# A product tile in two parts, the softmax four superblocks ahead, and other places for the x loads, in a dynamic convolution followed by a gated two-matmul block

## The chip, the cores and the metric

One core of a Trainium2 chip. The metric is the device time of one execution in microseconds (us); of the kernel before there are three runs.

## What is computed

The input x has 8 sequences of 4096 tokens with 192 channels; weight_gen has, for each token and each of 8 heads, 7 weights. A softmax is taken over the 7 weights; each output channel is the weighted sum of the channel at this token and the six before it (zeros before the start of a sequence). The result, 32768 tokens by 192, goes through a matmul to 2048 channels, the function h - tanh(h), and a matmul back to 192.

```python
w = np.exp(weight_gen - max); w = w / sum(w)
x_pad = concatenate([zeros((B, 6, D)), x], axis=1)
out = einsum('bshk,bskhg->bshg', w, x_unf)     # x_unf: 7 shifted copies of x_pad
h = out.reshape(B * S, D) @ w_in
return (h - tanh(h)) @ w_out
```

## The kernel before

The tokens are cut into 32 superblocks (SBs) of 1024: partition p holds 8 tokens in a row (J = 8) and, ahead of them, the six before (HALO). NSB = 4 SBs make a sequence, so SBs 0, 4, 8, ... 28 start one; their first partition has no tokens before it and gets zeros in its halo.

Each SB goes through these steps:

- `load_wg` (L96) and `load_x` (L106) bring the softmax weights (128 x 448 numbers) and x (128 rows of 14 x 192 numbers, 10,752 bytes each) through SP's queue. `rows(p0, p1, ...)` issues the load of partitions p0 to p1; `no_halo` (L123) fills the halo of partition 0 with zeros.
- `softmax_exp` (L144, ACT), `softmax_sum` (L157, DVE) and `softmax_norm` (L172, DVE) give the weights `wsm`.
- `products` (L221) multiplies x by the weights for the seven taps. In the steady part this is all on GpSimd (POOL): taps 0 and 1, then 2 to 5, then 6, into one tile `pr` with two buffers.
- `dma_sum` (L213) is an accumulating DMA that POOL issues: it adds taps 3 to 5 onto 0 to 2 (the first sum, issued between the second and the third product, SUM_FIRST). For the SBs in TWO_SUMS a second one (`second_sum`, L289) follows, behind the first product of the next SB. SBs 2 to 4 (PART) have one sum of two taps; SBs 0 and 1 have none.
- `conv_sums` (L294, TensorE) transposes and adds what is left of the taps: four groups of 24 small matmuls after one sum, two groups after two sums. `conv_out` (L322, ACT) copies the result out.
- `gemm1` (L349): sixteen steps f; in each the first matmul, tanh on ACT (L367), subtraction on DVE (L368). `out_stream` (L376) is the second matmul, whose pairs are spread over the steps of the next loop, and `store_out` (L402) copies and stores its result.

The order of the work is written out by hand: the main loop (L568) goes over n = 1 to 31 and, within it, over the steps f = 0 to 15. In loop n the first matmul of SB n, the second matmul of SB n-1, the transposes of SB n+1 (at f = 13 and 14), the products of SB n+2 (issued at f = 1), the softmax of SB n+3 and the loads of x of SB n+3 (at f = X_AT = 7, ordered behind that step's subtraction) and of the weights of SB n+4 stand. Each engine runs its own instructions in this order; a DMA queue likewise issues in order, and an issue that waits holds those behind it. Buffers are given by pools: x_t, the softmax tiles and `pr` have two each.

Of the kernel before, what the change touches and what calls it, by code (L numbers as in the profile page):

```python
# [8 lines left out]
FP32 = mybir.dt.float32  # L9
BF16 = mybir.dt.bfloat16  # L10
# [6 lines left out]
def kernel(  # L17
# [8 lines left out]
    nc = tc.nc  # L26

    B, S, D = x.shape
    H, K = weight_gen.shape[2], weight_gen.shape[3]
    G = D // H  # L30
    F = moe_w_in.shape[1]
    P = nc.NUM_PARTITIONS
# [8 lines left out]
    NTOT = B * NSB  # L41
    NFT = F // P
    NC = D // R
    PLAIN = (0, 1)
    PART = tuple(range(2,5))
    TWO_SUMS = tuple([n for n in range(13,NTOT) if n%3])
    SUM_FIRST = tuple(range(5,32))
    SCALE_TWICE = True
    assert S % TOK == 0 and D % R == 0 and F % P == 0
    assert NFT == 2 * J, "one token block of the second matmul per pair of f tiles"  # L50

    const = ctx.enter_context(tc.tile_pool(name="const", bufs=1))
    xpool = ctx.enter_context(tc.tile_pool(name="xpool", bufs=2))
    wgpool = ctx.enter_context(tc.tile_pool(name="wgpool", bufs=2))
    ppool = ctx.enter_context(tc.tile_pool(name="ppool", bufs=2))
    cpool = ctx.enter_context(tc.tile_pool(name="cpool", bufs=2))
    tpool = ctx.enter_context(tc.tile_pool(name="tpool", bufs=3))
    gpool = ctx.enter_context(tc.tile_pool(name="gpool", bufs=2))
# [25 lines left out]
    last_exp = {}  # L84
    last_conv = {}
    first_halo = {}

    def order(inst, other, reason):
        tc.add_manual_dep(
# [16 lines left out]
    def load_x(n, behind=None):  # L106
        b, s = divmod(n, NSB)
        s0 = s * TOK

        x_t = xpool.tile([P, HALO + J, D], FP32, name="x_t")  # L110

        def rows(p0, p1, r0=0, r1=HALO + J):
            first = x[0, 0:1]
            return nc.sync.dma_start(
                out=x_t[p0:p1, r0:r1, :],
                in_=bass.AP(
                    tensor=first.tensor,
                    offset=first.offset + (b * S + s0 + p0 * J - HALO + r0) * D,
                    ap=[[J * D, p1 - p0], [D, r1 - r0], [1, D]],
                ),  # L120
            )

        def no_halo():  # L123
            nc.sync.dma_start(
                out=x_t[0:1, 0:HALO, :],
                in_=zero[:].rearrange("o (h d) -> o h d", h=1).to_broadcast([1, HALO, D]),
            )


        if n == 0:  # L130
            rows(0, P, HALO, HALO + J)
            rows(16, P, 0, HALO)
            rows(1, 16, 0, HALO)
            no_halo()
        else:
            dma = rows(0, P)
            if behind is not None:
                order(dma, behind, "order of the loads")
            if s == 0:

                no_halo()
        x_of[n] = x_t

    def softmax_exp(n):  # L144
        wg_t = wg_of.pop(n)
        e_t = wgpool.tile([P, J, H, K], FP32, name="e_t")
        last_exp[0] = nc.scalar.activation(  # L147
            out=e_t[:].rearrange("p j h k -> p (j h k)"),
            in_=wg_t[:].rearrange("p j h k -> p (j h k)"),
            func=ACT.Exp,  # L150
        )
        e_of[n] = e_t

    def softmax_tile():
        return wgpool.tile([P, J, H, K], FP32, name="wsm")

    def softmax_sum(n, j0=0, j1=J):  # L157

# [10 lines left out]
            zr_of[n] = wgpool.tile([P, J * H], FP32, name="zr")  # L169
        nc.vector.reciprocal(zr_of[n][:, j0 * H : j1 * H], zsum_of[n][:, j0 * H : j1 * H])  # L170

    def softmax_norm(n, bank):  # L172

        wsm = softmax_tile()
        zr_v = bank[:, 512 - J * H : 512]
        nc.vector.reciprocal(zr_v, zsum_of[n][:])  # L176

        def finish():
            scale(nc.vector, wsm[:], e_of[n], zr_v)
            wsm_of[n] = (wsm, None, None, None)  # L180

        return finish

    def softmax_norm_ramp(n, bank):
# [25 lines left out]
            zr.rearrange("p (n o) -> p n o", o=1).to_broadcast([P, J * H, K]),  # L210
        )

    def dma_sum(pr, k0, k1, src0, src1, step=1):  # L213
        nc.gpsimd.dma_start(  # L214
            out=pr[:, k0:k1].rearrange("p k j d -> p k (j d)"),
            in_=pr[:, src0:src1:step].rearrange("p k j d -> p k (j d)"),
            accum_op=mybir.AluOpType.add,
            max_dma_last_dim=2 * J * D,
        )

    def products(n, taps=None, sums=None, hooks={}):  # L221

        x_t = x_of.pop(n)
        wsm, wsm_v, e_t, zr = wsm_of.pop(n)
        if e_t is not None:
            scale(nc.gpsimd, wsm[:], e_t, zr[:])

        pr = ppool.tile([P, K, J, D], BF16, name="pr")
        x_v = x_t[:]
        step = x_v.ap[0]  # L230

        def mul(eng, k0, k1, j0=0, j1=J):

            w = wsm_v if eng is nc.vector else wsm[:]
            nj = j1 - j0
            return eng.tensor_mul(  # L236
                pr[:, k0:k1, j0:j1, :].rearrange("p k j (h g) -> p k (j h) g", h=H),
                bass.AP(
                    tensor=x_v.tensor,
                    offset=x_v.offset + (k0 + j0) * D,  # L240
                    ap=[step, [D, k1 - k0], [G, nj * H], [1, G]],
                ),
                w[:, j0:j1]
                .rearrange("p j h (k o) -> p k (j h) o", o=1)[:, k0:k1]
                .to_broadcast([P, k1 - k0, nj * H, G]),
            )

        def parts(*ks):
            return [[pr[:, k] for k in ks]] * NC

        if taps is not None:
            for eng, k0, k1, j0, j1 in taps:
                m = mul(eng, k0, k1, j0, j1)
                if j1 == 1:
                    first_halo[0] = m
                if k0 in hooks:
                    hooks[k0]()
            prods_of[n] = parts(*sums)
            return

        if n in PLAIN:
            mul(nc.gpsimd, 0, 3)
            mul(nc.gpsimd, 3, 5)
            mul(nc.gpsimd, 5, K)
            prods_of[n] = parts(*range(K))
        elif n in PART:
            mul(nc.gpsimd, 0, 2)
            mul(nc.gpsimd, 2, 4)
            dma_sum(pr, 0, 2, 2, 4)
            mul(nc.gpsimd, 4, K)  # L270
            prods_of[n] = parts(4, 5, 6, 0, 1)
        else:
            mul(nc.gpsimd, 0, 2)
            second_sum(n - 1)
            mul(nc.gpsimd, 2, 6)
            if n in SUM_FIRST:
                dma_sum(pr, 0, 3, 3, 6)
            mul(nc.gpsimd, 6, K)
            if n not in SUM_FIRST:
                dma_sum(pr, 0, 3, 3, 6)  # L280
            if n in TWO_SUMS:
                to_sum[n] = pr
                prods_of[n] = parts(0, 1)
            else:
                prods_of[n] = parts(6, 0, 1, 2)
            if n == NTOT - 1:
                second_sum(n)

    def second_sum(n):  # L289

        if n in to_sum:
            dma_sum(to_sum.pop(n), 0, 2, 2, K, 4)

    def conv_sums(n, parts, pcs, home=None):  # L294

# [53 lines left out]
    def gemm1(n, f):  # L349
# [17 lines left out]
        last_act[0] = nc.scalar.activation(out=th[:], in_=ph_f, func=ACT.Tanh)  # L367
        last_sub[0] = nc.vector.tensor_sub(gt[:], ph_f, th[:])  # L368
        g_of.setdefault(n, []).append(gt)

    LAST = (NTOT - 1) * J
    half = {}
# [139 lines left out]
    for c in range(NC):  # L512
# [2 lines left out]
    nc.sync.dma_start(out=w_in[R:P, :, FA:F], in_=w_in[0:R, :, FA:F])  # L515
    products(
        1,
        taps=[(V, 0, 1, 0, J), (V, 1, 2, 0, J), (G_, 2, 5, 0, J), (G_, 5, 7, 0, J)],
        sums=range(K),
        hooks={2: load_w_out},  # L520
    )
    conv(0, (0, 1), (2,))
    softmax_exp(2)
    load_x(2)
    softmax_norm_ramp(2, obank[0])
    products(2)

    def some(sums, m):
        for _ in range(m):
# [26 lines left out]

    STEADY = dict(pairs=(4, 12, 0, 16, 0, 16, 0, 16, 0, 6, 10, 6, 10, 8, 8, 16), t1=(14, 8), t2=(13, 0), scale=14, sums=(2, 5))
    FIRST = dict(pairs=(4, 12, 0, 16, 1, 15, 0, 16, 0, 16, 0, 13, 3, 0, 16, 16), t1=(15, 2), t2=(11, 10), scale=15, sums=(1, 2, 3, 4, 8, 10))
    X_AT = 7

    def transposes(n, chunks):
        pcs = []
# [2 lines left out]
        conv_out(n, (chunks,), pcs)  # L565
        return pcs[0]

    for n in range(1, NTOT):  # L568
        more = n < NTOT - 1
        finish = None  # L570
        plan = FIRST if n == 1 else STEADY
        for f in range(NFT):
            gemm1(n, f)
            if n == 1:
                if f == 1:
                    load_wg(5)
# [5 lines left out]
                        step(m, h * JH, (h + 1) * JH)  # L582
                if f == 5:
                    wsm_of[3] = (softmax_tile(), None, e_of[3], zr_of[3])
                    products(3)
            elif f == 1:
                if n + 3 < NTOT:
                    softmax_exp(n + 3)
                if n + 4 < NTOT:
                    load_wg(n + 4)  # L590
                if n < NTOT - 2:
                    products(n + 2)
            if n > 1 and n + 3 < NTOT:
                for h, at in enumerate(plan["sums"]):
                    if f == at:
                        softmax_sum(n + 3, h * JH, (h + 1) * JH)
            if f == X_AT and n + 3 < NTOT:
                load_x(n + 3, last_sub[0])
            done = 0
            for chunks, at in sorted((((0, 1), plan["t2"]), ((2,), plan["t1"])), key=lambda c: c[1]):  # L600
                if more and at[0] == f:
                    out_pairs(at[1] - done)
                    done = at[1]
                    pc = transposes(n + 1, chunks)
                    if chunks == (2,) and n + 3 < NTOT:
                        finish = softmax_norm(n + 3, pc[:, 0])
            if finish is not None and f >= plan["scale"]:
                finish()
                finish = None
            out_pairs(plan["pairs"][f] - done)  # L610

    gemm2_last(0, 0, J)
# [34 lines left out]
```

The softmax here doesn't subtract the row's maximum and nothing guards it: scores larger than these inputs give would overflow.

## Time and profile before

| What | Value |
|---|---|
| Median of 3 runs | 754.72 us (754.22 to 755.33) |
| The profiled execution | 753.12 us |
| Its span, first to last instruction | 751.4 us |
| Granted TensorE clock over the span | 0.994 |
| TensorE / VectorE / ScalarE / GpSimd busy | 97% / 88% / 85% / 89% |
| First x product on GpSimd of an SB (128x3072), mean | 5.92 us |
| x load, issue to landing, median (least, most) | 6.1 us (5.5, 7.3) |
| Tap sum of three taps / of two, issue to landing, median | 9.9 / 6.8 us |

PE is TensorE, PEld its weight loads, DVE is VectorE, ACT is ScalarE, POOL is GpSimd and SP is SyncE, which here only issues DMAs; a "q" behind a name is the engine's sequencer. L with a number is the line of the kernel. A row of a group or of the timeline names engine, operation, output <- inputs, shape, and how many instructions; in square brackets stands how long the engine had been idle before, and who ended the wait. Busy time of an engine that is not the last to be ready costs nothing.

### The profile page before, as it was taken

To read this page: it belongs to the slowest core of one execution; us is meant where nothing else is said; L and a number is where in the kernel's file an instruction comes from. 1 tells how busy PE (TensorE), PEld (TensorE's weight loads), DVE (VectorE), ACT (ScalarE), POOL (GpSimd) and SP (SyncE) were. 2 spreads that over 40 slices of the span, in tenths; PEclk is the share of its full clock that TensorE was granted. 3 is DMA by queue.
4 is the path that set the end of the run, shared out by engine and by line. 5 is a ranking of instruction groups with operands and counts; after the bars stand their busy time and mean duration, and the time that the engine had idled before them with its cause. 6 is when DMAs were issued, how large, how long until landed. Compare 5 with 4: busy or idle time off the path is not lost.

```text
span 751.4 us, 30497 instructions
## 1 busy us (share of the span) xinstructions
PE 725.4 (97%) x13928; PEld 567.6 (76%) x13928; DVE 664.6 (88%) x655; ACT 638.8 (85%) x872; POOL 668.9 (89%) x150
## 2 busy tenths in 40 slices
PE   3899999999999999999999999999999699999998
PEld 2477887787887777777777777777787577777777
DVE  7999889998889998999999999999989589998983
ACT  4888888888888888898989899898989588988883
POOL 7999999999999999999999999999999988999000
PEclk9999999999999999999999999999999899999999
DMA  8944526665655567785796777579668658673412
GB/s 234 242 111 107 171 109 173 187 181 126 191 149 170 169 170 160 202 196 163 196 229 151 180 203 185 169 196 215 173 157 192 180 139 189 183 177 85 113 44 86
DMA packets 32511, 124.99 MB, mean 166 GB/s; under 512 B 4495, under 2 KB 9343, under 8 KB 28414
## 3 DMA queue, kind: packets, MB, share of 16 engines
q0 software_dynamic: 17664, 46.01, 35.7%
q1 hardware_dynamic: 14718, 77.03, 27.6%
q8 instruction: 109, 1.79, 0.9%
q14 instruction: 20, 0.16, 0.1%
HBM read 54.52 MB, written 25.17 MB: 106 GB/s over the span
## 4 chain that ended last, share of the span: by engine, by line
PE 49%; DMA 4%; POOL 4%; issue 0%; ACT 0%; DVE 0%; POOLq 0%; DVEq 0%
PE obank L389 23%; PE ph L354 22%; DMA pr<-pr 4%; POOL pr L236 4%; PE pc L311 2%; PE po L432 1%; ACT th L367 0%; DVE wsm L207 0%; POOL pr L214 0%; ACT convT L337 0%; DVE pc L176 0%; DVE out_sb L446 0%; ACT ot L445 0%; DVE gt L368 0%; POOLq L214 0%
## 5 line engine op out<-in xcount | busy, mean ns | idle before, releaser
L368 DVE TENSOR_TENSOR gt<-ph,th 128x1024 bf16<-128x1024 f32 x512 | 603.1, 1218 | 66.8 <-ACT th L367 66.2
L236 POOL TENSOR_TENSOR pr<-x_t,wsm 128x3072 bf16<-128x3072 f32 (+3 forms) x95 | 629.7, 6816 | 8.1 <-PE obank L389 3.4
L367 ACT ACTIVATE th<-ph 128x1024 f32<-128x1024 f32 x512 | 506.8, 1026 | 71.1 <-PE ph L354 66.9
L354 PE MATMUL ph<-convT,w_in 64*128 64x512 bf16 x3072 | 407.3, 380 | 5.0 <-DVE gt L368 3.2
L389 PEld LDWEIGHTS <-gt 64*128 64x128 bf16 x7936 | 353.0, 94 | 73.0 <-issue 11.7
L389 PE MATMUL obank<-w_out,gt 64*128 64x192 bf16 x7936 | 399.5, 243 | 0.6 <-issue 0.5
L354 PEld LDWEIGHTS <-w_in 64*128 64x128 bf16 x3072 | 171.5, 95 | 82.7 <-issue 12.2
L408 ACT ACTIVATE out_sb<-obank 128x192 f32<-128x192 f32 x248 | 82.4, 332 | 12.9 <-PE obank L389 10.4
L214 POOL DMA_DIRECT2D pr<-pr x43 | 54.9, 1276 | 20.4 <-DMA pr<-pr 11.0
L311 PEld LDWEIGHTS <-pr 64*128 64x128 bf16 x2664 | 51.9, 102 | 24.1 <-POOL pr L236 10.2
L311 PE MATMUL pc<-ident,pr 64*128 64x64 bf16 x2496 | 50.7, 194 | 16.6 <-POOL pr L236 10.1
L337 ACT ACTIVATE convT<-pc 128x1024 bf16<-128x1024 f32 (+1 forms) x62 | 50.5, 816 | 7.3 <-PE pc L311 6.7
L161 DVE TENSOR_REDUCE zsum<-e_t 128x32 f32<-128x224 f32 (+1 forms) x61 | 23.6, 387 | 3.0 <-ACT e_t L147 3.0
L147 ACT ACTIVATE e_t<-wg_t 128x448 f32<-128x448 f32 x32 | 18.2, 569 | 7.3 <-DMA wg_t<-in_weight_gen_dram 7.3
L207 DVE TENSOR_TENSOR wsm<-e_t,pc 128x448 f32<-128x448 f32 x28 | 17.4, 621 | 3.3 <-POOL pr L236 0.5
L176 DVE RECIPROCAL pc<-zsum 128x64 f32<-128x64 f32 x28 | 15.4, 551 | 0.1
L432 PE MATMUL po<-w_out,gt 64*128 64x192 bf16 x256 | 11.2, 243 | 0.0
L236 DVE TENSOR_TENSOR pr<-x_t,obank 128x1536 bf16<-128x1536 f32 (+4 forms) x8 | 10.3, 1349 | 0.6 <-ACT wsm L199 0.6
L432 PEld LDWEIGHTS <-gt 64*128 64x128 bf16 x256 | 10.8, 93 | 0.0
L446 DVE TENSOR_TENSOR out_sb<-po,ot 128x192 f32<-128x192 f32 x8 | 2.9, 358 | 9.0 <-ACT ot L445 9.0
L445 ACT ACTIVATE ot<-po 128x192 f32<-128x192 f32 x8 | 2.6, 331 | 7.3 <-PE po L432 7.3
L467 POOL DMA_DIRECT2D w_in<-in_moe_w_in_dram x4 | 2.5, 628 | 3.0 <-ACT e_t L147 3.0
(19 smaller groups left out, 18.3 us busy)
## 6 DMA issues: line engine op xcount, KB each, us to landing
x_t<-in_x_dram SPq DMA_DIRECT2D x31, 1344.0 KB, 6.0
pr<-pr POOLq DMA_DIRECT2D x27, 1152.0 KB, 9.9
out_dram<-out_sb SPq DMA_DIRECT2D x31, 768.0 KB, 3.4
pr<-pr POOLq DMA_DIRECT2D x16, 768.0 KB, 6.8
wg_t<-in_weight_gen_dram SPq DMA_DIRECT2D x32, 224.0 KB, 6.8
x_t<-in_x_dram SPq DMA_DIRECT2D x1, 768.0 KB
w_out<-in_moe_w_out_dram POOLq DMA_DIRECT2D x1, 768.0 KB, 9.6
out_dram<-out_sb SPq DMA_DIRECT2D x4, 192.0 KB, 3.9
```

Source lines behind the costliest of these rows:

```text
L147: last_exp[0] = nc.scalar.activation(out=e_t[:].rearrange("p j h k -> p (j h k)"), in_=wg_t[:].rearrange("p j h k -> p (j h k)"), func=ACT ...
L161: nc.vector.reduce_sum(out=zsum_of[n][:, j0 * H : j1 * H], in_=e_of[n][:, j0:j1].rearrange("p j h k -> p (j h) k"), axis=AX.X,)
L214: nc.gpsimd.dma_start(out=pr[:, k0:k1].rearrange("p k j d -> p k (j d)"), in_=pr[:, src0:src1:step].rearrange("p k j d -> p k (j d)"), acc ...
L236: return eng.tensor_mul(pr[:, k0:k1, j0:j1, :].rearrange("p k j (h g) -> p k (j h) g", h=H), bass.AP(tensor=x_v.tensor, offset=x_v.offset ...
L311: nc.tensor.matmul(pc[r][:, col : col + R] if home else pc[:, r, col : col + R], lhsT=prods[c][gi][r * R : (r + 1) * R, 2 * j : 2 * j + 2] ...
L337: last_conv[0] = nc.scalar.activation(out=out, in_=pc[:, :, 0:cols].rearrange("p r (cj t) -> p r cj t", t=R), func=ACT.Copy,)
L354: nc.tensor.matmul(ph[:, r, :], lhsT=w_in[r * R : (r + 1) * R, c, f * P : (f + 1) * P], rhs=convT[r * R : (r + 1) * R, c, :], start=(c == ...
L367: last_act[0] = nc.scalar.activation(out=th[:], in_=ph_f, func=ACT.Tanh)
L368: last_sub[0] = nc.vector.tensor_sub(gt[:], ph_f, th[:])
L389: mm = nc.tensor.matmul(po[:, 0:D], lhsT=g_of[n][f][r * R : (r + 1) * R, col : col + P], rhs=w_out[r * R : (r + 1) * R, f, :], start=(r == ...
L408: last_act[0] = nc.scalar.activation(out=out_sb[:, j, :], in_=po[:, 0:D], func=ACT.Copy)
L432: nc.tensor.matmul(po[:, r, 0:D], lhsT=g_of[n][f][r * R : (r + 1) * R, col : col + P], rhs=w_out[r * R : (r + 1) * R, f, :], start=(f == 0 ...
```

## The change

The product tile is split in two. `pa` holds taps 0 to 3 (KA = 4) and has three buffers, `pb` holds taps 4 to 6 and has one. The products become three instructions: taps 0 and 1 (KH = 2), taps 2 and 3, then 4 to 6. The first sum adds `pb` onto taps 0 to 2 of `pa` and is issued behind the last product; the second sum of the SB before is issued behind the second product. The second half of the products, `rest`, is written at step f = 9, though on POOL it follows the first half directly. The set of SBs with two sums loses 13 and 14.

The exponential is written in place over its input, so the softmax tiles need fewer names; they have three buffers, and `wsm` a pool of its own with four. From loop 4 on the softmax runs for SB n+4 instead of n+3 (loop 4 does two).

The load of x of SB n+3 is now issued at f = 1 and ordered behind the first product of SB n+2 (before: at f = 7, behind a subtraction). For the SBs that start a sequence it consists of the zeros, the rest of partition 0's row, and one load of partitions 1 to 127, instead of one load of 128 partitions and then the zeros over it. HELP is empty, so the branch under it makes no instruction.

```diff
-    TWO_SUMS = tuple([n for n in range(13,NTOT) if n%3])
-    SUM_FIRST = tuple(range(5,32))
+    KA, KH = 4, 2
+    TWO_SUMS = (16, 17, 19, 20, 22, 23, 25, 26, 28, 29, 31)
+    AHEAD = 4
+    HELP = ()
+    HELP_AT = 9
...
-    wgpool = ctx.enter_context(tc.tile_pool(name="wgpool", bufs=2))
-    ppool = ctx.enter_context(tc.tile_pool(name="ppool", bufs=2))
+    wgpool = ctx.enter_context(tc.tile_pool(name="wgpool", bufs=3))
+    papool = ctx.enter_context(tc.tile_pool(name="papool", bufs=3))
+    pbpool = ctx.enter_context(tc.tile_pool(name="pbpool", bufs=1))
+    wspool = ctx.enter_context(tc.tile_pool(name="wspool", bufs=4))
...
-            dma = rows(0, P)
+            if s == 0:
+                no_halo()
+                rows(0, 1, HALO)
+            dma = rows(1 if s == 0 else 0, P)
             if behind is not None:
                 order(dma, behind, "order of the loads")
-            if s == 0:
-
-                no_halo()
...
-        e_t = wgpool.tile([P, J, H, K], FP32, name="e_t")
         last_exp[0] = nc.scalar.activation(
-            out=e_t[:].rearrange("p j h k -> p (j h k)"),
+            out=wg_t[:].rearrange("p j h k -> p (j h k)"),
...
-            mul(nc.gpsimd, 0, 2)
-            second_sum(n - 1)
-            mul(nc.gpsimd, 2, 6)
-            if n in SUM_FIRST:
-                dma_sum(pr, 0, 3, 3, 6)
-            mul(nc.gpsimd, 6, K)
...
+        x_after[n + 1] = mul(nc.gpsimd, 0, KH, 0, J - 1 if n in HELP else J)
+        mul(nc.gpsimd, KH, KA)
+        second_sum(n - 1)
+
+        def rest(ph=None):
...
+            if n in PART:
+                dma_sum(pa[:, 0:2], pa[:, 2:4])
+            mul(nc.gpsimd, KA, K)
+            if n in PART:
+                prods_of[n] = parts(4, 5, 6, 0, 1)
             else:
-                prods_of[n] = parts(6, 0, 1, 2)
-            if n == NTOT - 1:
-                second_sum(n)
+                dma_sum(pa[:, 0:3], pb[:, 0:3])
+                if n in TWO_SUMS:
+                    to_sum[n] = pa
+                    prods_of[n] = parts(0, 1)
+                else:
+                    prods_of[n] = parts(3, 0, 1, 2)
+                if n == NTOT - 1:
+                    second_sum(n)
...
+    def emit_x(m):
+        if m < NTOT:
+            load_x(m, x_after.pop(m, None))
...
+        soft = [m for m in (n + 3,) * (n <= AHEAD) + (n + 4,) * (n >= AHEAD) if m < NTOT]
         for f in range(NFT):
-            gemm1(n, f)
+            ph = gemm1(n, f)
...
-                if n + 3 < NTOT:
-                    softmax_exp(n + 3)
-                if n + 4 < NTOT:
-                    load_wg(n + 4)
-                if n < NTOT - 2:
-                    products(n + 2)
+                if soft and n != AHEAD + 1:
+                    softmax_exp(soft[0])
+                if n + 2 < NTOT:
+                    rest = products(n + 2)
...
-            if f == X_AT and n + 3 < NTOT:
-                load_x(n + 3, last_sub[0])
+            if f == NFT - 1 and n in (AHEAD - 1, AHEAD):
+                load_wg(n + 5)
+            if f == (9 if n == 1 else HELP_AT) and n + 2 < NTOT:
+                rest(ph)
+            if f == (9 if n == 1 else 1):
+                emit_x(n + 3)
+                if soft and n != AHEAD and soft[0] + 1 < NTOT and n > 1:
+                    load_wg(soft[0] + 1)
```

## The prediction

> **What bounds the kernel now.** I read the page's busy times and chain, then the engines by stages, the GpSimd timeline and the DMA queues.
>
> ```profile
> PE 725.4 (97%) x13928; PEld 567.6 (76%) x13928; DVE 664.6 (88%) x655; ACT 638.8 (85%) x872; POOL 668.9 (89%) x150
> ...
> PE 49%; DMA 4%; POOL 4%; issue 0%; ACT 0%; DVE 0%; POOLq 0%; DVEq 0%
> ```
>
> TensorE is busy for 97%; the chain ends through it, with one stretch through POOL and its DMAs. The stages say where (PE, PEld, DVE, ACT, POOL, clock, DMA share, GB/s):
>
> ```profile
> 110.00:310.00 200.00, 199.19 (x3948) 158.97 (x3945) 180.97 (x178) 176.59 (x241) 194.45 (x40) 1.00 0.64 170
> 310.00:530.00 220.00, 219.89 (x4151) 170.39 (x4148) 203.44 (x201) 197.05 (x271) 213.76 (x47) 1.00 0.74 188
> 530.00:620.00 90.00, 83.95 (x1496) 65.74 (x1494) 75.67 (x75) 73.23 (x99) 84.20 (x18) 0.96 0.68 170
> 620.00:715.00 95.00, 95.00 (x1854) 74.49 (x1852) 84.77 (x80) 84.29 (x116) 71.52 (x18) 1.00 0.62 147
> ```
>
> Between 110 us and the tail TensorE stops once for long, 6.05 us in the third row (a tap sum, 597 us), where its clock is 0.96 too. The steady part is TensorE's, but POOL is nearly as full, 194.45 of 200. POOL's rhythm in a superblock (SB) with one sum:
>
> ```profile
> 329.34 1.28 POOL L214 DMA_DIRECT2D pr<-pr  x1 [0.30 <-POOL pr L236]
> 330.16 19.99 POOL L236 TENSOR_TENSOR pr<-x_t,wsm 128x1536 bf16<-128x1536 f32 x3
> 350.45 1.29 POOL L214 DMA_DIRECT2D pr<-pr  x1 [0.30 <-POOL pr L236]
> ```
>
> That is 350.45 - 329.34 = 21.1 us (19.99 of products, 0.30 of wait, 0.82 of issue), and 0.8 more with a second sum. TensorE's is 21.7 (output stores of two SBs issued at 555.67 and 577.40 us). POOL has about 0.6 us an SB to spare: what holds it for tens of microseconds holds TensorE. So the change is decided by how POOL is fed, and I read the DMA queue that carries x (packets, MB, share of 16 engines):
>
> ```profile
> q1 hardware_dynamic: 14718, 77.03, 27.6%
> ```
>
> **What the skill says.** All in the page "DMA: Bandwidth & Descriptors". Section "Why a DMA increments its semaphore by 16 and not by 1": a DMA from SP is split over the largest number k of engines, at most 16, that divides the count of the slowest dimension on both sides; it names 128 partitions as 16 and 127 as 1, and only those k engines post a completion. The trace of before agrees where it can. The shapes give 3968 + 255 packets of x, 4096 of weights, 3968 + 512 of output, 192 of w_in and 48 of zeros, 13,039 in all; 14,718 less these is 1,679 completions. The 110 DMAs would make 1,760 with 16 each; with 16 for 101 of them, 15 for the 15-row load and 6 for each of the eight zero fills (six rows) it is 1616 + 15 + 48 = 1,679. This does not prove the case of 127: no load of before has a count above 16 that 16 doesn't divide. Section "Specifications": about 27 GiB/s for one engine. Here 77.03 MB in 27.6% of 16 x 751.4 us is 23.2 GB/s while carrying. Section "Queues, rings and completion order": one engine takes a queue's descriptors in order and alternates between queues by packet; the trace of before shows no transfer long enough to test it.
>
> **The change, part by part.**
>
> 1. x loads of the SBs that start a batch (n = 4, 8, ... 28, seven of them). Before: one load of 128 rows, then zeros over the halo, for which SP waited until the load had landed (40.1 us in seven waits, on no path). After: zeros, the rest of row 0, then rows 1 to 127 in one DMA. With k = 1 its 127 x 10,752 B = 1.366 MB go through one engine. Prices of the bare transfer: 47.1 us at 27 GiB/s (an estimate from the skill), 58.8 us at the 23.2 GB/s above. I take 51.3: the packet records of the trace show 10,752 B rows at a median of 404 ns, and the 23.2 contains other queues' turns. To this come the fixed part, 2.3 us (the shortest x load landed after 5.5 us, less 8 rows x 0.404), and the tap sums that share that engine: a three-tap sum has 24 descriptors of 3,072 B per engine at 282 ns in the records, 6.8 us; a two-tap sum 4.6. Landing after issue: n = 4 58.2 us; n = 8 to 20 60.5 (one sum); n = 24 and 28 65.1 (a second sum is issued inside too).
>
> 2. When it is issued: ordered behind the first product of SB n-1 on POOL (before: behind a subtract at f = 7). POOL wants x of n after the rest of SB n-1: 21.1 - 5.6 = 15.5 us later. An ordinary load (median 6.0 us) fits under that, and costs nothing; without that cover it would cost its 6. The seven do not fit: POOL stalls 58.2 - 15.5 = 42.7, then 4 x 45.0, then 2 x 48.8 (0.8 us goes to the second sum), together 320 us. POOL's lead doesn't help, since the load isn't issued before POOL itself gets to n-1.
>
> 3. Who waits behind it. On SP, the load of x of n+1 waits for the first product of n, and behind it wait the weights for the next exponential and an output store. On engine 0, the weights issued after the 127 rows land after them, so ACT's exponential of the next loop stands until about 62 us after the issue, with every tanh behind it. This lies beside POOL's stall: after it TensorE needs 4 x 21.7 = 87 us to the next such exponential, and the next is released a POOL cycle later, 129 us. The softmax weights for n+3 are made by 62 + 40 = 102 us, POOL wants them at 60.5 + 63.3 = 124: 21 us to spare.
>
> 4. POOL's products: three of 2, 2 and 3 taps instead of 2, 4 and 1. Same columns, 19.99 us. The first sum is issued after the last product, not before it, 3.4 us (one 128x1536 product) later: hidden by the stall, otherwise 3.4 of latency. Three first-part buffers take away the 1.2 us waits for PE ahead of L236 (3.4 in all). The single second part waits for the first sum, 10 us, under 11.2 us of products: nothing, or up to 1 us an SB if sums take 12. For SBs 2 to 4 it waits for TensorE's transposes; those of SB 2 end at 60.4 us, before POOL needs it at 64: nothing.
>
> 5. Second sums: those of 13 and 14 go. TensorE transposes 4 groups instead of 2 there: 4 x 24 = 96 more matmuls at 0.41 us per 16 (L311 in the timeline), 2.5 us, under POOL's stalls.
>
> 6. Softmax four ahead, exponential in place: the same 32 exponentials (0.57 us) and scalings, moved to earlier loops; nothing in sum, at most the two extra of loop 4, 2 us of ACT and DVE once.
>
> **The sum, along POOL.** First product of SB 3 ends at 58.6 us as before. Each cycle of four is landing + 5.6 + 3 x 21.1, with 1.6 more from n = 16 for two second sums: n = 4: 127.1, to 185.7; 8 and 12: 129.4 each, to 444.5; 16 and 20: 131.0 each, to 706.5; 24 and 28: 135.6 each, to 977.7, the first product of SB 31. Two products more (5.6 + 8.8) and 0.3: 992.4. First sum lands 10.4 later (as 689.37 to 699.79), the second about 8: 1010.8. From the last transposes to the end it was 751.4 - 709.7 = 41.7: span 1052.5. The profiled execution took 753.12, 1.7 over its span, and the median of three 754.72, 1.6 over that; so 1055.8, say 1055 us.
>
> **Rivals.**
> A, the forecast: one engine. 1055.
> B, which ends faster: the 127 rows are split over 16 engines, eight rows each. Then a load lands in 6 to 7 us, under 15.5 of cover, and what is left is POOL's slack: 6.05 us of stall and 0.04 x 90 = 3.6 of clock go, 2.5 of transposes come: 753.1 - 9.6 + 2.5 = 746, as a median 748. It decides at a landing of 15.5 us: below that the seven loads cost nothing. For it: the trace never shows 127 rows. Against: the skill names 127 as one engine, and the completions counted above follow its rule.
> C: one engine, but undisturbed by the sums and at 27 GiB/s: every landing 49.4 us, so 8.8 + 4 x 11.1 + 2 x 15.7 = 85 less: 970. At 23.2 GB/s, sums on top: 7 x 7.5 = 52 more: 1107. These are A's own ends.
> D: the waits fall in series. After the 6 us stall of before, TensorE took 1.50 us where it takes 0.84 (16 matmuls of L389 at 597.86). If that lasts for two loops after each hold, 40 us x 0.8 = 32 exceed the 21 to spare by 11, and with the exponential some 17 per cycle: 7 x 17 = 119, 1170. Against: before, the speed was back within 8 us.
>
> **Numbers.** A with its ends 0.86, B 0.08, D 0.04, 0.02 for a mixture that ends near no change. Range 970 to 1110, A's ends; B and D stay out. A difference under 0.2% can't be told from no change here. Faster 0.08, same 0.01, slower 0.91.
>
> **What would show it.** Seven gaps of 40 to 50 us on POOL ahead of the first product of 4, 8, ... 28, ended by the DMA of x; ACT waiting for wg_t in the loop after; the landing's maximum at 55 to 65 us while its median stays near 6; four times 21 us between the gaps. If the landing's maximum is under 10 us, A is wrong and B holds. If the gaps are as forecast and TensorE still ends later than POOL's sum, D.

## The result, and the profile after

The changed kernel takes 1066.91 us (median of 4 runs, 1065.11 to 1067.16) against 754.47 of the kernel before in the same comparison: ratio 1.414, 95% interval 1.411 to 1.417. The profiled execution took 1065.11 us, its span is 1063.3. The forecast was 1055 us, range 970 to 1110. Ratios here and below are of fast runs only: a run over 1.5% above the fastest of its kernel counts as slow.

Page of the changed kernel, busy times and the chain that ended last:

```profile
PE 749.7 (71%) x14024; PEld 579.1 (54%) x14024; DVE 666.2 (63%) x655; ACT 641.7 (60%) x872; POOL 665.7 (63%) x149
...
POOL 50%; another core or an unknown queue 26%; PE 11%; issue 5%; DMA 4%; DVE 2%; ACT 1%; POOLq 0%; SPq 0%; ACTq 0%; DVEq 0%
```

POOL and DVE do the same work as before in microseconds (665.7 for 668.9, 666.2 for 664.6), spread over 312 us more; the chain has moved from TensorE to POOL. TensorE's busy time rose by 24 us (749.7 for 725.4). Only 2.5 of them are the 96 extra matmuls, by their rate (an estimate); its granted clock was 0.862 over the span instead of 0.994, and 0.89 from 250 to 270 us, right after a hold, against 1.00 from 270 to 318. The "unknown queue" is 26% of 1063.3, some 276 us: the x loads, as the list of waits shows (who waited for whom: us in total, times, longest):

```profile
ACT wg_t L151 <- DMA wg_t<-in_weight_gen_dram: 279.5, 9, 46.6
POOL pa L252 <- DMA x_t<-in_x_dram: 278.5, 7, 48.2
PE obank L414 <- ACT out_sb L433: 269.2, 7, 46.2
...
POOL pa L252 <- issue: 42.4, 1, 42.4
```

POOL's waits for x are six stalls of these, and a seventh, at 74 us, stands under "issue": 320.9 us together (the row of seven holds a small one too). ACT waits nearly as long for the softmax weights, and TensorE nearly as long for ACT. The GpSimd timeline shows one of the seven and the superblocks up to the next:

```profile
182.31 11.72 POOL L252 TENSOR_TENSOR pa<-x_t,wsm 128x3072 bf16<-128x3072 f32 x2
193.47 8.84 POOL L252 TENSOR_TENSOR pb<-x_t,wsm 128x4608 bf16<-128x4608 f32 x1
202.62 1.28 POOL L218 DMA_DIRECT2D pa<-pb  x1 [0.30 <-POOL pb L252]
249.49 11.20 POOL L252 TENSOR_TENSOR pa<-x_t,wsm 128x3072 bf16<-128x3072 f32 x2 [45.59 <-DMA x_t<-in_x_dram]
...
270.10 11.71 POOL L252 TENSOR_TENSOR pa<-x_t,wsm 128x3072 bf16<-128x3072 f32 x2
...
312.33 11.71 POOL L252 TENSOR_TENSOR pa<-x_t,wsm 128x3072 bf16<-128x3072 f32 x2
...
379.55 11.20 POOL L252 TENSOR_TENSOR pa<-x_t,wsm 128x3072 bf16<-128x3072 f32 x2 [45.64 <-DMA x_t<-in_x_dram]
```

The first product of SB 7 ends at about 187.9 and releases the load of SB 8; POOL starts on it at 249.49, 61.6 us later. 379.55 - 249.49 = 130.1 us is one cycle of four SBs. The DMA queue with x (packets, MB, share):

```profile
q1 hardware_dynamic: 14620, 76.99, 21.3%
```

The shapes again give 13,039 data packets, so 1,581 completions (the packet records of the trace hold 1,581 packets of 4 bytes in this queue): 98 fewer than before. Seven loads that posted 16 now post 1 (-105), and seven loads of the rest of row 0 are new with 1 each (+7): -98. So the load of 127 rows ran on one engine, as the Trainium skill, "DMA: Bandwidth & Descriptors", section "Why a DMA increments its semaphore by 16 and not by 1", has it: a transfer gets the largest number of engines up to 16 that divides its rows. The packet records show the same: from 192 to 204 us, rows of 10,752 B follow one another without overlap, five in 2 us, each 0.40 us.

### The profile page after: what moved, and what is told of

It reads as the page before. It is cut to its first block, busy times and chain, and to the rows that moved or that the text cites. A ratio compares the mean times of both kernels' runs of the same rounds, so it can differ in the third digit from the quotient of the medians.

```text
span 1063.3 us, 30685 instructions
## 1 busy us (share of the span) xinstructions
PE 749.7 (71%) x14024; PEld 579.1 (54%) x14024; DVE 666.2 (63%) x655; ACT 641.7 (60%) x872; POOL 665.7 (63%) x149
## 4 chain that ended last, share of the span: by engine, by line
POOL 50%; another core or an unknown queue 26%; PE 11%; issue 5%; DMA 4%; DVE 2%; ACT 1%; POOLq 0%; SPq 0%; ACTq 0%; DVEq 0%
POOL pa L252 27%; POOL pb L252 20%; PE obank L414 5%; PE ph L378 5%; POOL pa L218 3%; DMA pa<-pa 2%; PE po L457 1%; DVE gt L392 1%; DMA wg_t<-in_weight_gen_dram 1%; DMA x_t<-in_x_dram 1%; PE pc L335 1%; ACT th L391 1%; DVE pb L252 0%; DVE pa L252 0%
## 5 line engine op out<-in xcount | busy, mean ns | idle before, releaser
L414 PE MATMUL obank<-w_out,gt 64*128 64x192 bf16 x7936 | 410.4, 248 | 270.6 <-ACT out_sb L433 269.2
L252 POOL TENSOR_TENSOR pa<-x_t,wsm 128x3072 bf16<-128x3072 f32 (+1 forms) x63 | 357.8, 5864 | 321.2 <-DMA x_t<-in_x_dram 278.5
L252 POOL TENSOR_TENSOR pb<-x_t,wsm 128x4608 bf16<-128x4608 f32 (+2 forms) x33 | 277.6, 8411 | 2.8 <-PE pc L335 2.8
L151 ACT ACTIVATE wg_t<-wg_t 128x448 f32<-128x448 f32 x32 | 18.3, 571 | 279.5 <-DMA wg_t<-in_weight_gen_dram 279.5
L335 PEld LDWEIGHTS <-pa 64*128 64x128 bf16 x2400 | 47.2, 102 | 33.4 <-issue 24.5
L335 PE MATMUL pc<-ident,pa 64*128 64x64 bf16 x2304 | 48.1, 195 | 24.4 <-DMA pa<-pa 17.7
L218 POOL DMA_DIRECT2D pa<-pb x27 | 34.7, 1287 | 8.8 <-POOL pb L252 8.5
L218 POOL DMA_DIRECT2D pa<-pa x14 | 21.0, 1498 | 9.1 <-DMA pa<-pb 8.2
L165 DVE TENSOR_REDUCE zsum<-wg_t 128x32 f32<-128x224 f32 (+1 forms) x61 | 23.7, 388 | 2.9 <-ACT wg_t L151 2.9
L211 DVE TENSOR_TENSOR wsm<-wg_t,pc 128x448 f32<-128x448 f32 x28 | 17.3, 621 | 2.8
L180 DVE RECIPROCAL pc<-zsum 128x64 f32<-128x64 f32 x28 | 15.5, 553 | 1.3 <-ACT convT L361 1.1
L457 PE MATMUL po<-w_out,gt 64*128 64x192 bf16 x256 | 11.2, 243 | 0.0
L457 PEld LDWEIGHTS <-gt 64*128 64x128 bf16 x256 | 10.8, 93 | 0.0
(25 smaller groups left out, 36.7 us busy)
```

Source lines behind the costliest of these rows:

```text
L151: last_exp[0] = nc.scalar.activation(out=wg_t[:].rearrange("p j h k -> p (j h k)"), in_=wg_t[:].rearrange("p j h k -> p (j h k)"), func=AC ...
L165: nc.vector.reduce_sum(out=zsum_of[n][:, j0 * H : j1 * H], in_=e_of[n][:, j0:j1].rearrange("p j h k -> p (j h) k"), axis=AX.X,)
L218: return nc.gpsimd.dma_start(out=out.rearrange("p k j d -> p k (j d)"), in_=in_.rearrange("p k j d -> p k (j d)"), accum_op=mybir.AluOpTyp ...
L252: return eng.tensor_mul(prod(k0, k1)[:, :, j0:j1].rearrange("p k j (h g) -> p k (j h) g", h=H), bass.AP(tensor=x_v.tensor, offset=x_v.offs ...
L335: nc.tensor.matmul(pc[r][:, col : col + R] if home else pc[:, r, col : col + R], lhsT=prods[c][gi][r * R : (r + 1) * R, 2 * j : 2 * j + 2] ...
L414: mm = nc.tensor.matmul(po[:, 0:D], lhsT=g_of[n][f][r * R : (r + 1) * R, col : col + P], rhs=w_out[r * R : (r + 1) * R, f, :], start=(r == ...
```

## The experiments

Each is compared with runs of the kernel before that were made beside it. "Split kernel" below is the changed kernel with the first edit.

**1. Rows 1 to 127 in loads of 112 and 15.**

```diff
-            dma = rows(1 if s == 0 else 0, P)
+            dma = rows(16 if s == 0 else 0, P)
             if behind is not None:
                 order(dma, behind, "order of the loads")
+            if s == 0:
+                rows(1, 16)
```

> The changed kernel, but in the superblocks that start a sequence rows 1 to 127 come in two loads, of 112 and of 15 rows, instead of one of 127. Theory (127 rows run on one DMA engine, landing about 61 us after issue): both new loads spread over 16 and 15 engines and land in 6 to 8 us, under the 15.5 us that GpSimd gives them, so all seven stalls go: 748 us, between 742 and 756. Rival (the time is lost to something else in the change: the ordering of the loads behind GpSimd's product, the single second-part buffer, sums that come later): it stays above 1000 us.

Measured: 763.22 us, ratio 1.0128 (1.0113 to 1.0143). All seven stalls are gone: POOL's products on `pa` wait 3.6 us in all, where they waited 321.2 in the changed kernel. The DMA queue shows the engines (page, group of products and DMA queue):

```profile
L254 POOL TENSOR_TENSOR pa<-x_t,wsm 128x3072 bf16<-128x3072 f32 (+1 forms) x63 | 356.6, 5827 | 3.6 <-PE obank L416 2.6
...
q1 hardware_dynamic: 14830, 77.00, 30.4%
```

Less 13,039, that is 1,791 completions, 112 more than before: 16 + 15 + 1 in each of seven superblocks instead of 16. So of the 312 us, 1066.9 - 763.2 = 304 hang on the count of 127. But 748 was not reached: what is left of the change costs 1.3%, outside the expected range. The waits of TensorE (first the kernel before, then this one) show a part of it:

```profile
PE pc L311 <- DMA pr<-pr: 6.0, 1, 6.0
...
PE obank L389 <- issue: 0.5, 2, 0.3
```

```profile
PE obank L416 <- issue: 10.7, 7, 2.2
```

The one 6 us stall for a tap sum went, as forecast; seven waits of 0.4 to 2.2 us came in its place that nothing in the list releases. In the packet records the five largest of these waits, 9.6 us together, end 1.2 to 1.6 us after a 16 KB packet of the instruction queue, of which one comes about every 7 us (109 in the span). As I read it, TensorE had run out of instructions; that is not shown. With TensorE's busy time, 730.2 us for 725.4, the change of these waits makes 9.0 of the 9.9 us by which the span is longer.

**2. Rows 1 to 127 in loads of 5 and 122: two engines instead of one.**

```diff
+            dma = rows(6 if s == 0 else 0, P)
...
+            if s == 0:
+                rows(1, 6)
```

> The changed kernel, but with loads of 122 and 5 rows instead of 127. The largest divisor of 122 up to 16 is 2, so theory puts 61 rows on each of two engines: 61 x 0.405 + 2.3 of fixed time + 4.6, 6.8 or 11.4 of tap sums, 32 to 38 us to landing, less 15.5 of cover: stalls of 16 to 23 us; along GpSimd 127 us per four superblocks become 101 to 109: about 870 us (850 to 890). Rival (a load whose rows 16 does not divide is slow as such, whatever its largest divisor): near 1065. Rival (rows are shared out over 16 engines whatever their number): 748.

Measured: 886.86 us (one run). The stalls are 19.3 to 23.3 us from the second on; GpSimd timeline:

```profile
199.15 11.20 POOL L254 TENSOR_TENSOR pa<-x_t,wsm 128x3072 bf16<-128x3072 f32 x2 [20.55 <-DMA x_t<-in_x_dram]
...
736.73 11.20 POOL L254 TENSOR_TENSOR pa<-x_t,wsm 128x3072 bf16<-128x3072 f32 x2 [22.71 <-DMA x_t<-in_x_dram]
```

The largest divisor sets the number of engines: neither 1065 nor 748. The completions agree:

```profile
q1 hardware_dynamic: 14662, 76.99, 26.1%
```

That is 1,623, or 56 fewer than before: 2 + 5 + 1 in each of seven superblocks instead of 16. With two engines a row still took 0.40 to 0.42 us in the records.

**3. Rows 1 to 127 in loads of 3 and 124: four engines.** The same edit with 4 in place of 6.

> The changed kernel, but with loads of 124 and 3 rows instead of 127. The largest divisor of 124 up to 16 is 4, so theory puts 31 rows on each of four engines: 31 x 0.405 + 2.3 + 4.6 to 11.4 of tap sums, 19 to 26 us to landing, stalls of 4 to 10 us on GpSimd in the seven places; along GpSimd 783 us at most, and as TensorE's own rate gives 763, some of it is hidden: 775 us (763 to 785). Rival (slow whenever 16 does not divide the rows): near 887 or above.

Measured: 817.15 us, ratio 1.0865 (1.0835 to 1.0896). The direction is right, the size is not. The completions, 1,623 again, are those of 4 + 3 + 1 engines. POOL waits 73.0 us for x, and the stalls scatter:

```profile
82.25 11.20 POOL L254 TENSOR_TENSOR pa<-x_t,wsm 128x3072 bf16<-128x3072 f32 x2 [7.81 <-DMA x_t<-in_x_dram]
...
276.90 11.20 POOL L254 TENSOR_TENSOR pa<-x_t,wsm 128x3072 bf16<-128x3072 f32 x2 [13.59 <-DMA x_t<-in_x_dram]
367.01 11.20 POOL L254 TENSOR_TENSOR pa<-x_t,wsm 128x3072 bf16<-128x3072 f32 x2 [5.68 <-DMA x_t<-in_x_dram]
```

The records say where my sum failed: it put a row at 0.405 us. Of the rows that no other data overlapped, half took over 0.69 us in the load that POOL waited for until 276.90, but only 0.40 in that until 367.01; by load the medians run from 0.40 to 0.69, and the stall is long where the rows are slow. With one engine and with two the median was 0.40 in every load. Why rows on four engines are slower at times was not tried.

**4. The kernel before with the load of 127 rows alone.**

```diff
-            dma = rows(0, P)
+            if s == 0:
+                no_halo()
+                rows(0, 1, HALO)
+            dma = rows(1 if s == 0 else 0, P)
             if behind is not None:
                 order(dma, behind, "order of the loads")
-            if s == 0:
-
-                no_halo()
```

> The kernel before, with this one edit of the change: zeros, the rest of row 0, then one load of rows 1 to 127, in the superblocks that start a sequence. Theory: the same seven stalls alone make nearly the whole loss. The load can be issued as soon as the x buffer is free, one product (5.6 us) earlier than in the changed kernel, so each cycle is some 5.6 us shorter: about 1025 us (990 to 1065). Rival (the other parts of the change cause a good part of the loss, or hide some of it by their deeper buffers): below 950 or above 1090.

Measured: 1076.11 us (one run), above the expected range: this edit alone makes a loss a little larger than the whole change's. POOL waits 331.8 us for x. Timelines of GpSimd and of SP's queue:

```profile
511.42 16.64 POOL L236 TENSOR_TENSOR pr<-x_t,wsm 128x3072 bf16<-128x3072 f32 x2 [50.73 <-DMA x_t<-in_x_dram]
```

```profile
439.15 0.34 SPq L412 DMA_DIRECT2D out_dram<-out_sb  x1
439.58 0.86 SPq L124 DMA_DIRECT2D x_t<-zero  x1
440.50 7.45 SPq L114 DMA_DIRECT2D x_t<-in_x_dram  x2
```

I expected the load at the start of SB 15's products (436.9). It goes out 11 us later, at 447.7, in the middle of them: in this kernel it stands behind an output store and behind a subtraction at f = 7, both of which hang on TensorE, which the last stall had held. Ordering it behind POOL's product, as the change does, is the better place once POOL is late.

**5. The weights' load ahead of the x load.**

```diff
-                emit_x(n + 3)
                 if soft and n != AHEAD and soft[0] + 1 < NTOT and n > 1:
                     load_wg(soft[0] + 1)
+                emit_x(n + 3)
```

> The changed kernel, with the softmax weights' load ahead of the x load in SP's order, so that the weights no longer queue behind the 127 rows. Theory (the scalar engine's seven waits of 46 us lie beside GpSimd's, which set the pace): the waits on wg_t go from 279 us to under 30, and the time hardly moves, 1060 to 1067. Rival (the two waits are in series, or the scalar engine's sets the pace): 15 us or more are won, up to 119.

Measured: 1065.55 us, ratio 1.4140 (1.4116 to 1.4164), not to be told from 1.414 of the changed kernel. ACT's waits in this run:

```profile
ACT out_sb L433 <- DMA out_dram<-out_sb: 235.7, 7, 44.7
...
ACT wg_t L151 <- DMA wg_t<-in_weight_gen_dram: 36.7, 3, 29.4
```

The wait for the weights went from 279.5 to 36.7 us, and the next transfer in the same queue, the output store, took its place: ACT must not overwrite out_sb before it has landed. The time stays because POOL's 320 us stay. This supports that the two holds lie side by side; as ACT was not freed from a hold altogether, it does not show what ACT alone would cost.

**6. The split kernel with second sums from 13 again.** TWO_SUMS gets 13 and 14.

> The kernel with loads of 112 and 15 rows (763.2 us), with second sums from superblock 13 again, as before the change. Theory (13 and 14 cost 96 matmuls of transposes, 2.5 us by their rate): 760.5 us. Rival (four groups of transposes also make TensorE wait for its instructions, which is where the rest went): 758 or less.

Measured: 759.21 us, ratio 1.0089 (1.0067 to 1.0111): 4.0 us less than the split kernel, or 2.9 by the two ratios, as the two were measured beside different runs of the kernel before. That lies between the two expectations. TensorE's waits for instructions on obank are 8.9 us here (10.7 before the edit). Some 2.5 us are the matmuls, by their rate.

**7. The split kernel with x loaded at f = 7 again.**

```diff
+            if f == (9 if n == 1 else 7):
+                if n == 1:
+                    emit_x(n + 3)
+                elif n + 3 < NTOT:
+                    load_x(n + 3, last_sub[0])
```

> The kernel with loads of 112 and 15 rows (763.2 us), with the x load back at step f = 7 behind that step's subtraction, as before the change; the weights stay at f = 1. In the 763 us kernel TensorE stands 10.7 us in seven waits that no semaphore explains (issue), each ending about 1.3 us after a block of its instructions was fetched by DMA; the kernel before has 0.5 us of them. Theory (the x load behind GpSimd's product, next to the tap sums, delays those fetches): these waits fall under 3 us and the time to 755 us. Rival (they come from where TensorE's instruction blocks end, not from the x load's place): the waits stay, 761 to 765.

Measured: 786.30 us (six runs). The ratio, 1.0360 (1.0295 to 1.0425), is of the three lowest, 774.69 to 784.52; the others took 788.07 to 791.50. My theory fell, on the far side. Waits of TensorE, and of POOL:

```profile
PE pc L337 <- issue: 15.0, 3, 6.9
PE obank L416 <- issue: 12.9, 12, 2.6
```

```profile
POOL pa L254 <- DMA x_t<-in_x_dram: 36.2, 13, 6.4
```

The waits for instructions did not go, so the x load's place is not what makes them. And POOL, which now runs ahead of TensorE, waits 36 us for loads that are tied to TensorE's step: putting x behind POOL's own product is a part of the change that pays.

**8. The kernel before with second sums from 16.** `range(13,NTOT)` becomes `range(16,NTOT)`.

> The kernel before, with second sums from superblock 16 instead of 13: this part of the change alone. TensorE gets 96 matmuls more (2.5 us), GpSimd two sum issues less (1.6 us), which may take part of the 6 us stall at 597 us away. Theory: the two nearly cancel, 752 to 757. Rival (four groups of transposes in 13 and 14 cost more than their matmuls, through waits for instructions): 758 or above.

Measured: 752.77 us (746.71 to 755.64, 14 runs), ratio 0.9995 (0.9969 to 1.0022): no difference that can be told. The 6 us stall is still there (5.5 us, now under issue).

**9. The kernel before with the first sum behind the last product.** `SUM_FIRST = ()`.

> The kernel before, with one part of the change alone: the first tap sum is issued behind the last product instead of ahead of it (SUM_FIRST empty). Each sum lands 3.4 us later, in a kernel whose two product buffers leave GpSimd little lead. Theory (the sum's place beside TensorE's transposes is what delays its instruction fetches in the 763 us kernel): its waits for issue on obank, 0.5 us before, rise over 5 us, and the time to 760 us or more. Rival (the later sum costs only latency): more and longer waits of TensorE for the sums, few for issue; 754 to 775.

Measured: 796.85 us, ratio 1.0571 (1.0544 to 1.0598), above both expectations. Waits of POOL and of TensorE:

```profile
POOL pr L214 <- DMA pr<-pr: 39.1, 10, 9.1
POOL pr L236 <- PE obank L389: 26.0, 13, 3.0
```

```profile
PE pc L311 <- DMA pr<-pr: 30.0, 5, 7.2
...
PE obank L389 <- issue: 1.6, 3, 1.0
```

Few waits for instructions on obank (1.6 us), so the sum's place alone does not make those either. What it makes is a full stop and go of POOL and TensorE: between the issue of the first sum and that of the second now lie only the 5.6 us of one product, where in the kernel before the 3.4 us of the last product lay there too; the sum takes 9.9 us to land, so POOL stands at the second issue. In the changed kernel this place costs POOL nothing because the second sum moved too, behind two products of 11.2 us: POOL's one wait for a sum there, 8.2 us, is the last of all, at 1010 us.

**10 to 12. The split kernel with more second sums.** TWO_SUMS is two of three SBs from 5, three of four from 5, three of four from 13.

```diff
+    TWO_SUMS = tuple(n for n in range(5, NTOT) if n % 3)
```

```diff
+    TWO_SUMS = tuple(n for n in range(5, NTOT) if n % 4)
```

```diff
+    TWO_SUMS = tuple(n for n in range(13, NTOT) if n % 4)
```

> The kernel with loads of 112 and 15 rows and second sums in two of three superblocks from 5 on (18 in all). From 11 to 13 such superblocks the time fell from 763.2 to 759.2, 2 us each. Theory (TensorE's transposes are still the limit and GpSimd has room, 21.6 us a superblock on average): five more give 749 us (746 to 752), below both kernels. Rival (GpSimd's lead is used up, as it is without three first-part buffers): 753 or above, with TensorE waiting for sums.

> As the run with sums in two of three superblocks, but in three of four (all from 5 on except 8, 12, ... 28): 21 second sums. Theory: TensorE 743, GpSimd's own end with its tail 744: 745 us (742 to 749). Rival (GpSimd becomes the bound): 750 or above.

> The kernel with loads of 112 and 15 rows and second sums in three of four superblocks from 13 on (15 in all). The run with three of four from 5 on lost 17 us at superblocks 5 to 7, where GpSimd had no lead yet, and had TensorE without a gap of over 1.2 us afterwards. Theory (begun at 13 the lead is there, so those 17 us go, and six more superblocks with four groups cost 1.25 to 2 us each): 753 us (750 to 756), level with the kernel before. Rival (the waits for instructions in the superblocks with four groups eat it up): 757 or above, as the 759 with 13 second sums.

Measured: 758.61 us (one of the six runs, the profiled one, took 773.83), ratio 1.0069 (1.0055 to 1.0084); 761.10, 1.0099 (1.0084 to 1.0113); 757.65, 1.0047 (1.0029 to 1.0065). None beats the kernel before. Three of four from 5, engines by stages (PE, PEld, DVE, ACT, POOL, clock, DMA share, GB/s):

```profile
60.00:166.00 106.00, 88.67 (x1663) 67.78 (x1655) 82.26 (x84) 77.82 (x106) 97.90 (x20) 0.93 0.64 158
166.00:700.00 534.00, 531.53 (x9992) 413.76 (x9994) 486.21 (x475) 474.38 (x651) 523.48 (x116) 1.00 0.79 186
```

```profile
PE pc L337 <- DMA pa<-pa: 18.4, 4, 12.9
```

From 166 to 700 us TensorE is full to 2.5 us, and its waits for instructions on obank are 0.3 us; but 17 us are lost before, where, as I read it, POOL has no lead yet. Begun at 13, that loss goes and the waits for instructions are back (10.2 us).

## Why the prediction was right, step by step

*One engine for 127 rows* (step 1): right, shown by the completions and by experiments 1, 2 and 4. Landing after issue was forecast at 60.5 us for SBs 8 to 20; for SB 8 it was 60.4 (issued at 188.5, last completion at 248.8), and 61.6 from POOL's release of the load to POOL's start. The tap sum did lengthen it: from 212 to 218 us, with only a last share of the sum left, rows and sum packets alternated, three of each in 2 us instead of five rows.

*POOL's stalls* (step 2): forecast 42.7, four times 45.0, twice 48.8, together 320 us; measured 42.4, 45.6, 45.6, 45.4, 45.3, 48.2 and 48.1, together 320.6. That the total agrees so closely is partly luck: the 1.1 us between 60.5 and 61.6 was left out, and so was 0.5 us of cover (16.0 instead of 15.5, from 187.9 to 203.9).

*What waits behind* (step 3): ACT stood for the weights seven times, 34 to 47 us each, beside POOL's stall. The records agree with the account of their place in the queue: behind SB 8's rows, 15 of the weights' completions came at 218.6 to 219.1 us and the last at 249.4, after the rows. That it costs nothing holds to a few us only, see below.

*Products and sums on POOL* (step 4): the period is 21.1 us as forecast. "Nothing" for the single second part of SBs 2 to 4 was off by one wait of 2.8 us, in SB 5, for TensorE's transposes of SB 4, which the first stall had made late.

*The end*: forecast 1052.5 for the span, 1063.3 measured. The first product of SB 31 ends at 985.8 instead of 977.7. The 2.8 us are a part of that; the rest is mis-sized terms in every cycle, 0.7 us in those with one sum (130.1 for 129.4) and 0.8 to 1.5 in those with second sums. A second sum costs POOL 1.25 us (22.37 from 529.95 to 552.32, against 21.12 from 270.10 to 291.22), not 0.8: in the timeline the product behind an issue starts before the issue's row ends and runs 0.5 us longer. Then the sum along POOL gives transposes of SB 31 at 1018.8, but they begin at 1021.5 with TensorE at work without a pause: at the very end it was TensorE, released by ACT at 915.7 and at work since then but for one pause of 1.7 us, that was last. That term was missing in the sum: 2.7 of the 10.8 us by which the span was off.

*The rivals*: B, loads spread over 16 engines, is excluded for 127 rows, and its price was wrong too. The split kernel has what B described, and takes 763, not 748. The 6 us stall did go; what I left out are the waits that nothing releases (10.7 us for 0.5), and TensorE's busy time was 730.2 us, where B's own terms give 725.4 - 3.6 + 2.5 = 724.3. These two make some 16 of the 17 us by which the profiled execution (763.1) missed B's 746; why the busy time rose is not shown. The place of the x load (experiment 7) and of the first sum (9) do not make these waits by themselves. They appear on obank in the split kernel with 11, 13, 15 and 18 second sums (10.7, 8.9, 10.2 and 6.2 us) and not with 21 (0.3), nor, to more than 1.6 us, in the kernels with the old product tile. What makes them stays open. C's two ends both fell: a row did take 0.40 us, and the sums did share the engine. D did not occur, though its first step did: TensorE was slower for a time after a hold, as its busy time and its clock show, but POOL waited for it only once, the 2.8 us.

## What to carry to other kernels

Before one row is split off a 128-partition transfer to save a wait, look at the largest divisor up to 16 of the count that is left: 127 rows put 1.37 MB on one engine of sixteen and turned a 6 us load into one of 61, while 112 and 15 rows did the same job without a stall. A transfer that is too long costs its length less the time between its issue and its need, 15.5 us here, and everything behind it in its queue waits too: moving one victim ahead only lets the next one show. It also matters which engine a load is ordered behind: tied to the consumer itself it came in time (experiment 1), tied to TensorE's step it came late (experiments 4 and 7).

## What the runs showed of the hardware

- The issue of a DMA can itself be held. Behind five of the seven loads of 127 rows, SP's row of the weights' load took 28 to 35 us, where its median in the kernel before is 0.43; in experiment 5 the output store, then next in the queue, took 27 to 33. The first of the five:

```profile
188.80 28.51 SPq L105 DMA_DIRECT2D wg_t<-in_weight_gen_dram  x1
217.40 4.34 SPq L437 DMA_DIRECT2D out_dram<-out_sb  x1
```

- A row of 10,752 B that no other data overlapped took 0.40 us on one engine and on two (medians of every load); on four engines the medians by load were 0.40 to 0.69. The completions counted are those of 16 + 15 engines for loads of 112 and 15 rows, 2 + 5 for 122 and 5, 4 + 3 for 124 and 3, and one for 127.
- A contiguous load of 1 x 1536 numbers (the rest of row 0) was one packet of 6,144 B with one completion: it was not spread at all.
- TensorE has waits in a straight program that nothing in the trace releases (experiment 1): seven of up to 2.2 us, the five largest of which ended 1.2 to 1.6 us after a 16 KB packet of the instruction queue had landed.
